# Two two-bank PSUM tiles become four one-bank tiles in a fused LSH-attention and feed-forward kernel

## The chip, the cores and the metric

One Trainium2 chip, one of its NeuronCores. The metric is the device time of one execution in microseconds (us), the median of three runs. A profiled execution gives the trace; its span runs from the first to the last instruction. Engines: PE is TensorE's matmul (PEld its weight load), DVE is VectorE, ACT is ScalarE, POOL is GpSimd, SP issues DMAs. A difference of 0.2% (1.5 us) is about what a measurement of this kernel can tell from no change.

## The reference

Attention over 2 batches of 8 heads, 768 positions of 64 numbers, in which a query sees only the keys of its own hash bucket, then two feed-forward layers over the 1536 tokens of width 512, with 2048 hidden columns each.

```python
bucket = sum((einsum(x, proj) > 0) * 2**k)                  # for q and for k, 6 bits
scores = where(q_bucket == k_bucket, q @ k.T / 8, -1e9)
x = softmax(scores) @ v                                     # [1536, 512]
h = x @ w_in;   x = maximum(0.01 * h, h) @ w_out            # layer 0
h = x @ w_in2;  y = maximum(h, 0) + alpha * minimum(h, 0)   # layer 1
out = y @ w_out2
```

## The kernel before

Every piece of work is an operation of a planner (`Plan`): it has a claim (its place in the wanted order), one or more engines that could do it with an estimated duration, and the buffers that it reads and writes. The planner simulates the engines with these estimates and emits the instructions in order of the starts that it finds. The semaphores are not the planner's: they are put in by the layer below it, tile by tile, from what each instruction reads and writes.

**Attention, about 0 to 247 us.** Eight pairs of heads. Of each pair 12 score blocks of 128 by 768 are multiplied by PE into the score tiles `sc` (L708), evicted by DVE with a minimum (L715) and raised by ACT (L718). Each score tile is `[128, 2, 512]`, two PSUM banks, and there are two of them in turn, slots 0 and 1 of the ring `s_ps`. Transposes and the product with v (L805, L814) follow. PSUM has eight banks: four in `s_ps`, two in `t_ps`, one in `o_ps`, one in `p_ps`.

**Feed-forward, about 247 us to the end.** Two layers, each in four quarters of the hidden columns (`fq`), each quarter for both batches. Weights and activations are split in a high and a low half of float16, so every product is three matmuls in a row into the same PSUM place, L1169, L1170 and L1171 in the function `three`. With 384 columns the hidden blocks `h` come out; seven products take the place of eight (`p1`, `p5`, `p2`, `p6`, `p3`, `p7`, `p4` in `h_steps`) in all but the first quarter of a layer. Six of the seven go to banks of `t_ps` or of `o_ps` and `p_ps`, and only `p2` takes a bank of `b_banks`. Then the leaky step (`leaky`), and `y_group`: four operations of three matmuls each (384 columns in layer 0, 512 in layer 1) add up one block of the second product of the quarter in a bank of `y_banks`.

**The banks that the change touches.** When the last score has been read, the two score slots are used for two tiles called `y`, of the score tiles' shape: `s_at2`. Bank 0 of tile k is `y_banks[k]`, bank 1 of tile k is `b_banks[k]`. Both lists are taken in turn. What is written there and who reads it:

- `y_banks`: the matmuls of `y_group`; read by ACT at L1300 in the first quarter, by DVE at L1303 in the others.
- `b_banks`: the product `p2`; read by DVE at L1214 (`sum_up`).
- `b_banks`: a small product at L948, by which a maximum over the partitions gets its way to all of them (`power`); read by DVE at L952. There are 16 for the weights, two for y and one for alpha.

The trace names all of these `y`. For the planner the two banks of a tile are already separate places (`Bank.use` names the bank as a span), so it gives them no common order.

Of the kernel before, what the change touches and what calls it, by code (L numbers as in the profile page):

```python
# [9 lines left out]
F32 = mybir.dt.float32  # L10
# [6 lines left out]
PSUM = bass.MemoryType.PSUM  # L17
# [30 lines left out]
class Slot:  # L48


    def __init__(self, pool, tag):
        self.pool, self.tag, self.bufs = pool, tag, []


class Buf:
# [12 lines left out]
    def put(self):  # L68

        if not self.ring:  # L70
            return None
        if self.slot:
            assert self.slot.bufs[-1] is self, self.slot.tag
            return None
        self.slot = self.ring.next()
        self.slot.bufs.append(self)
        return self.slot.bufs[-2] if len(self.slot.bufs) > 1 else None


class Ring:  # L80


    def __init__(self, slots):
        self.slots, self.n = list(slots), 0

    def next(self):
        self.n += 1
# [1 line left out]

    def new(self, shape, dtype, name):  # L90
        return Buf(self, lambda slot: slot.pool.tile(shape, dtype, tag=slot.tag, name=name))


class Op:
# [209 lines left out]
def lsh_attention_ffn_kernel(  # L304
# [36 lines left out]
    def pool(name, bufs, **kw):  # L341
        return ctx.enter_context(tc.tile_pool(name=name, bufs=bufs, **kw))

    def ring(name, n, tags=None, **kw):
        p = pool(name, 1, **kw)
        rings = [Ring([Slot(p, f"{tag}{k}") for k in range(n)]) for tag in tags or (name,)]
        return rings if tags else rings[0]

    def part(ring, *ks):
        return Ring([ring.slots[k] for k in ks])  # L350
# [1 line left out]
    const = pool("const", 1)  # L352
    xpool = pool("x", 1)

    s_ps = ring("ps_s", 2, space=PSUM)
    t_ps = ring("ps_t", 2, space=PSUM)
    o_ps = ring("ps_o", 1, space=PSUM)
    p_ps = ring("ps_p", 1, space=PSUM)
    w_r = ring("wraw", 1)
    raw_r = dict(zip("kq", ring("raw", 1, "kq")))  # L360
    nat_r = dict(zip("kq", ring("nat", 1, "kq")))
# [482 lines left out]
    class View:  # L844


        def __init__(self, buf, c0, n):
            self.buf, self.c0, self.n = buf, c0, n
# [64 lines left out]
    def bank(ring):  # L913
        return Bank(ring.new([128, 1, HALF], F32, "h"), 0)

    s_at2 = [part(s_ps, k).new([128, 2, 512], F32, "y") for k in range(2)]
    y_banks = Slots([Bank(b, 0) for b in s_at2])
    b_banks = Slots([Bank(b, 1) for b in s_at2])
    e_ps = Ring(o_ps.slots + p_ps.slots)
    wt, xs, gs = {}, {}, {}  # L920

# [503 lines left out]
```

## Time and profile before

| what | value |
|---|---|
| median of three runs | 746.21 us (745.81 to 746.28) |
| the profiled execution | 746.68 us, its span 744.7 us |
| mean granted TensorE clock | 0.99 |
| busy: PE | 709.6 us, 95% of the span |
| busy: DVE | 605.3 us, 81% |
| busy: ACT | 479.9 us, 64% |
| busy: POOL | 305.3 us, 41% |

The profiled execution is 0.47 us over the median, and 1.98 us of it lie outside the span. A busy PE is one with a matmul in flight: matmuls are pipelined, so that the row of one begins before the row of the last has ended.

### The profile page before, as it was taken

Reading aid. Unit: us, or ns where it says so; the run is one execution under the profiler, and the core shown is the slowest. Engines: PE = TensorE matmul, PEld = TensorE weight load, DVE = VectorE, ACT = ScalarE, POOL = GpSimd, SP = SyncE. Lnnn points to the kernel's source line nnn. Section 1 sums busy time; section 2 is a strip of 40 time slices with the busy share of each in tenths; the row PEclk is TensorE's granted clock in tenths of the full one; section 3 lists DMA queues with packets and bytes.
Section 4 is the critical chain, followed back from the end, with each engine's and each line's share of the span. In section 5 each row is a group of like instructions: output and inputs, shape, how many; then the busy total and the mean of one; then the engine's idle time right before and its main releaser. Section 6 shows DMA issues by size and latency. Waiting matters only on the chain.

```text
span 744.7 us, 13170 instructions
## 1 busy us (share of the span) xinstructions
PE 709.6 (95%) x4979; PEld 452.8 (61%) x4979; DVE 605.3 (81%) x1097; ACT 479.9 (64%) x907; POOL 305.3 (41%) x313
## 2 busy tenths in 40 slices
PE   7999999999995999999999999988999999999997
PEld 5778787788774665565565566554555555454443
DVE  6978787767989966789898879899989999788442
ACT  6988777788888675775656555654767655555430
POOL 2987756666373242141452224233133334221420
PEclk9999999999997999999999999999999999999999
DMA  7596686777757230330231313020032113010012
GB/s 212 132 207 155 159 196 149 153 156 132 119 121 198 85 114 1 114 114 28 86 114 58 101 70 114 28 85 2 22 107 99 57 58 114 1 56 1 28 43 99
DMA packets 109488, 72.41 MB, mean 97 GB/s; under 512 B 79137, under 2 KB 101665, under 8 KB 109425
## 3 DMA queue, kind: packets, MB, share of 16 engines
q1 hardware_dynamic: 109424, 71.57, 36.4%
q8 instruction: 39, 0.64, 0.4%
q14 instruction: 25, 0.20, 0.1%
HBM read 43.00 MB, written 3.15 MB: 62 GB/s over the span
## 4 chain that ended last, share of the span: by engine, by line
PE 77%; DVE 15%; ACT 3%; issue 2%; POOL 1%; DMA 1%; DVEq 0%; POOLq 0%; ACTq 0%
PE y L1169 11%; PE y L1171 11%; PE y L1170 11%; PE h L1169 8%; PE h L1171 8%; PE h L1170 8%; PE sc L708 7%; PE pp L734 4%; PE o L805 4%; PE o L814 4%; DVE ff L1094 3%; PE tp L537 2%; DVE s L715 2%; DVE x L1303 1%; PE bp L580 1%
## 5 line engine op out<-in xcount | busy, mean ns | idle before, releaser
L414 POOL TENSOR_TENSOR ff<-ff 128x384 f16<-128x384 f32 x128 | 136.3, 1079 | 323.6 <-ACT ff L1203 214.4
L1169 PE MATMUL y<-ff 128*128 128x384 f16 (+1 forms) x496 | 172.0, 347 | 8.7 <-DVE ff L1214 3.4
L1171 PE MATMUL y<-ff 128*128 128x384 f16 (+1 forms) x496 | 171.8, 346 | 0.0
L1170 PE MATMUL y<-ff 128*128 128x384 f16 (+1 forms) x496 | 171.8, 346 | 0.0
L1170 PEld LDWEIGHTS <-ff 128*128 128x128 f16 x912 | 89.2, 98 | 81.3 <-issue 15.2
L1169 PE MATMUL h<-ff 128*128 128x384 f16 x416 | 135.7, 326 | 2.4 <-DVE ff L1200 2.4
L1170 PE MATMUL h<-ff 128*128 128x384 f16 x416 | 135.6, 326 | 0.6 <-DVE ff L1094 0.6
L1171 PE MATMUL h<-ff 128*128 128x384 f16 x416 | 135.6, 326 | 0.0
L1171 PEld LDWEIGHTS <-ff 128*128 128x128 f16 x912 | 89.2, 98 | 70.0 <-issue 0.8
L1169 PEld LDWEIGHTS <-ff 128*128 128x128 f16 x912 | 89.2, 98 | 69.1 <-DVE biggest L952 0.8
L715 DVE TENSOR_SCALAR_CACHE_REDUCE s<-sc 128x768 f32<-128x768 f32 x96 | 90.3, 954 | 24.9 <-PE sc L708 19.4
L718 ACT ACTIVATE s<-s,mn 128x768 f32<-128x768 f32 x96 | 89.8, 937 | 4.5 <-DVE s L715 4.2
L1203 ACT CAST ff<-ff 128x384 f16<-128x384 f32 x128 | 64.8, 511 | 26.1 <-DVE ff L1200 24.2
L1303 DVE SCALAR_TENSOR_TENSOR x<-y,back,x 128x384 f32<-128x384 f32 (+1 forms) x84 | 55.8, 669 | 31.4 <-PE y L1171 30.5
L1210 ACT COPY ff<-h 128x384 f32<-128x384 f32 x72 | 34.3, 476 | 52.1 <-PE h L1171 51.2
L739 ACT COPY pt<-pp 128x384 f32<-128x384 f32 x96 | 45.6, 475 | 24.9 <-PE pp L734 24.4
L708 PE MATMUL sc<-ka,qa 128*128 128x384 f32 x192 | 56.9, 377 | 2.6 <-DVE s L715 2.4
L734 PE MATMUL pp<-ident,s 128*128 128x128 f32 x288 | 50.9, 286 | 4.2 <-ACT pt L739 3.4
L1094 DVE SCALAR_TENSOR_TENSOR ff<-ff,by 128x512 f16<-128x512 f32 (+2 forms) x54 | 50.6, 970 | 0.7 <-ACT ff L1092 0.7
L708 PE MATMUL sc<-kb,qb 76*128 76x384 f32 x192 | 49.8, 340 | 0.6 <-ACT kb L611 0.6
L1092 ACT ACTIVATE ff<-ff,by 128x512 f16<-128x512 f32 (+2 forms) x54 | 44.2, 865 | 6.8 <-DVE by L957 4.3
L814 PE MATMUL o<-pt,v 128*64 128x128 f32 x576 | 48.4, 276 | 0.0
(141 smaller groups left out, 1199.4 us busy)
## 6 DMA issues: line engine op xcount, KB each, us to landing
ff<-in_moe_w_in_dram SPq DMA_DIRECT2D x32, 512.0 KB
ff<-in_moe_w_out_dram SPq DMA_DIRECT2D x32, 512.0 KB
v<-in_v_dram SPq DMA_DIRECT2D x8, 384.0 KB
out_dram<-x SPq DMA_DIRECT2D x12, 256.0 KB
k<-in_k_dram SPq DMA_DIRECT2D x7, 384.0 KB
q<-in_q_dram SPq DMA_DIRECT2D x7, 384.0 KB
kb<-ka SPq DMA_DIRECT2D x14, 192.0 KB
qb<-qa SPq DMA_DIRECT2D x14, 192.0 KB
```

What stands on the lines that cost most here:

```text
L414: nc.gpsimd.tensor_tensor(out=o, in0=a, in1=b, op=ALU.subtract)
L708: nc.tensor.matmul(sc.t[:, h, 0:HALF], lhsT=o[a].t[0:rows, row:row + 128], rhs=o[b].t[0:rows, h * HALF:h * HALF + HALF], start=(n == 0), s ...
L715: plan.add(g, vec(1.03, lambda: nc.vector.tensor_scalar(out=s.t.rearrange("p (a b) -> p a b", a=2), in0=sc.t[:, :, 0:HALF], scalar1=FILL, ...
L718: plan.add(g, act(1.12, lambda: nc.scalar.activation(out=s.t, in_=s.t, func=AF.Exp, scale=-1.0, bias=mn.t[:, 0:1], accum_out=sm.t[:, t, j: ...
L734: nc.tensor.transpose(ps.t[:, c], s.t[:, k0:k0 + 128], ident.t)
L814: nc.tensor.matmul(ps.t[64 * j:64 * j + 64, t * 128:t * 128 + 128], lhsT=v32.t[:, j, c, :], rhs=whole(pt, t)[:, T * j + c], start=False, s ...
L1094: plan.add(claim, vec(0.2 + w * 0.00108, lambda: nc.vector.scalar_tensor_tensor(out=part(lo), in0=src(), scalar=c(), in1=part(hi), op0=ALU ...
L1169: nc.tensor.matmul(ps, lhsT=lh[0], rhs=rh[0], start=first, stop=False, skip_group_check=skip)
L1170: nc.tensor.matmul(ps, lhsT=lh[0], rhs=rh[1], start=False, stop=False, skip_group_check=skip)
L1171: nc.tensor.matmul(ps, lhsT=lh[1], rhs=rh[0], start=False, stop=last, skip_group_check=skip)
L1203: plan.add(claim, act(0.51, lambda: nc.scalar.copy(out=gh.ap(), in_=g.ap(F32))), [g.use()], [gh.use()])
L1303: plan.add(claim, vec(0.69 if l else 0.56, lambda: nc.vector.scalar_tensor_tensor(out=a(), in0=ps.ap(w), scalar=c(), in1=a(), op0=ALU.mult ...
```

## The change

The two two-bank tiles are given up. The score tiles get a pool of their own, `ps_s`, which is released when the first of the new tiles is made; then a second pool, `ps_f`, opens on the same four banks, with four tiles of one bank each. The first two are `y_banks`, the other two `b_banks`. `reuse_waits="tile"` says that a tile of the new pool waits for the users of the score tile on its own bank, not for all the pool's users. For the planner, the first use of each of the four comes behind the last uses of both score tiles (`Whole`, through `Ring.before`).

```diff
-        return self.slot.bufs[-2] if len(self.slot.bufs) > 1 else None
+        return self.slot.bufs[-2] if len(self.slot.bufs) > 1 else self.ring.before
...
+class Whole:
+    def __init__(self, ring):
+        self.ring = ring
+    @property
+    def uses(self):
+        return [use for slot in self.ring.slots for use in slot.bufs[-1].uses]
+
+class Later:
+    def __init__(self, make):
+        self.make, self.pool = make, None
+    def tile(self, *args, **kw):
+        self.pool = self.pool or self.make()
+        return self.pool.tile(*args, **kw)
...
-    s_ps = ring("ps_s", 2, space=PSUM)
     t_ps = ring("ps_t", 2, space=PSUM)
     o_ps = ring("ps_o", 1, space=PSUM)
     p_ps = ring("ps_p", 1, space=PSUM)
+    s_pool = tc.alloc_tile_pool(name="ps_s", bufs=1, space=PSUM)
+    s_ps = Ring([Slot(s_pool, f"ps_s{k}") for k in range(2)])
+
+    def single():
+        s_pool.release()
+        return ctx.enter_context(tc.tile_pool(name="ps_f", bufs=1, space=PSUM, reuse_waits="tile"))
+
+    f_pool = Later(single)
...
-    s_at2 = [part(s_ps, k).new([128, 2, 512], F32, "y") for k in range(2)]
-    y_banks = Slots([Bank(b, 0) for b in s_at2])
-    b_banks = Slots([Bank(b, 1) for b in s_at2])
+    f_at = [Ring([Slot(f_pool, f"ps_f{k}")], Whole(s_ps)).new([128, 512], F32, "y") for k in range(4)]
+    y_banks, b_banks = (Slots([Bank(b, 0) for b in f_at[k:k + 2]]) for k in (0, 2))
```

On every engine the instructions stand in the same order before and after (10,249 of them, waits aside): nothing is moved, added or left out. What differs is which semaphore 114 of the instructions wait for. Two places on PE show it.

The first is near 423 us, in layer 0. `y_3630` is the tile of banks 0 and 1 before; after, `y_3958` is a tile for y and `y_3634` one for products. `ff_3921` holds weights, `ff_3200` and `ff_3702` the operands of `p2`. Before:

```order
L1171 MATMUL y_3630<-ff_3852,ff_3921 128x384
L1169 LDWEIGHTS ff_3702
L1169 MATMUL y_3630<-ff_3200,ff_3702 128x384
L1170 LDWEIGHTS ff_3702
L1170 MATMUL y_3630<-ff_3200,ff_3702 128x384
L1171 LDWEIGHTS ff_3702
L1171 MATMUL y_3630<-ff_3200,ff_3702 128x384
L1169 LDWEIGHTS ff_3702
L1169 MATMUL y_3630<-ff_3200,ff_3702 128x384 [waits DVE_49]
```

After, with the line numbers 28 higher:

```order
L1199 MATMUL y_3958<-ff_3856,ff_3925 128x384
L1197 LDWEIGHTS ff_3706
L1197 MATMUL y_3634<-ff_3200,ff_3706 128x384 [waits DVE_49]
L1198 LDWEIGHTS ff_3706
L1198 MATMUL y_3634<-ff_3200,ff_3706 128x384
L1199 LDWEIGHTS ff_3706
L1199 MATMUL y_3634<-ff_3200,ff_3706 128x384
L1197 LDWEIGHTS ff_3706
L1197 MATMUL y_3634<-ff_3200,ff_3706 128x384
```

The first row ends a `y_group`, the rest is `p2`, in two halves of three matmuls. Before, the second half waited for DVE's read of the y block (L1303), which is in the other bank of the tile. After, the wait stands at the first half, and it is for an earlier reader of the products' own bank.

The second place is near 698 us, in layer 1, where two operations of a `y_group` (512 columns) follow the last half of a `p2`. Before:

```order
L1171 MATMUL y_3630<-ff_3615,ff_3702 128x384
L1169 LDWEIGHTS ff_3742
L1169 MATMUL y_3630<-ff_3921,ff_3742 128x512
L1170 LDWEIGHTS ff_3742
L1170 MATMUL y_3630<-ff_3921,ff_3742 128x512
L1171 LDWEIGHTS ff_3742 [waits Pool_49]
L1171 MATMUL y_3630<-ff_3921,ff_3742 128x512
L1169 LDWEIGHTS ff_3797 [waits Activation_49]
L1169 MATMUL y_3630<-ff_3921,ff_3797 128x512 [waits DVE_49]
```

After:

```order
L1199 MATMUL y_3634<-ff_3619,ff_3706 128x384
L1197 LDWEIGHTS ff_3746
L1197 MATMUL y_3958<-ff_3925,ff_3746 128x512 [waits DVE_49]
L1198 LDWEIGHTS ff_3746
L1198 MATMUL y_3958<-ff_3925,ff_3746 128x512
L1199 LDWEIGHTS ff_3746 [waits Pool_49]
L1199 MATMUL y_3958<-ff_3925,ff_3746 128x512
L1197 LDWEIGHTS ff_3801 [waits Activation_49]
L1197 MATMUL y_3958<-ff_3925,ff_3801 128x512
```

Before, the second operation of the y block waited for DVE's read of the product (L1214) in the other bank. After, the y block waits once, at its first matmul, for the last reader of its own bank. On DVE and ACT the readers change in the same way: before, a reader waited for the last matmul that had been issued into either bank of its tile, after for the last one into its own bank.

One wait becomes later. The first `y` tile to be written is that of alpha's small product (L948, near 225 us). Before, it stood on the banks of score slot 1 and waited for the last but one score eviction. After, the tiles of the new pool take the banks in the order in which they are first used, so this one gets a bank of slot 0, and waits for the last score eviction.

## Rows read from the trace of the kernel before

**Rows 1.** Windows by stage: length, then each engine's busy time (count), clock, DMA.

```profile
332.00:470.00 138.00, 135.35 (x830) 81.07 (x829) 118.94 (x197) 78.80 (x138) 46.89 (x44) 1.00 0.25 79
470.00:540.00 70.00, 64.25 (x367) 35.55 (x365) 64.56 (x108) 42.22 (x66) 18.62 (x20) 1.00 0.12 37
540.00:610.00 70.00, 69.91 (x381) 37.11 (x380) 64.33 (x107) 44.27 (x78) 23.64 (x21) 1.00 0.26 85
610.00:744.70 134.70, 126.99 (x660) 64.33 (x658) 88.44 (x149) 58.26 (x107) 37.63 (x39) 1.00 0.14 48
```

**Rows 2.** PE's waits from 290 us on: waiter, releaser, total us, times, longest.

```profile
PE y L1169 <- DVE ff L1214: 3.4, 5, 0.7
PE y L1169 <- DVE x L1303: 3.1, 5, 1.0
PE h L1169 <- DVE ff L1200: 2.4, 2, 2.0
PE y L1169 <- DVE biggest L952: 1.1, 3, 0.4
PE y L1169 <- DVE y_max L952: 0.4, 1, 0.4
```

**Rows 3.** Timeline 418.5 to 426 us: start, duration, instruction, idle before and its releaser.

```profile
418.59 0.36 PE L948 MATMUL y<-dg,ones 128*128 128x128 f32 x1
...
419.49 0.29 DVE L952 TENSOR_REDUCE biggest<-y 128x1 f32<-128x128 f32 x1 [0.55 <-PE y L1171]
419.83 0.32 PE L1169 MATMUL y<-ff 128*128 128x384 f16 x1 [0.38 <-DVE biggest L952]
...
422.11 0.33 PE L1171 MATMUL y<-ff 128*128 128x384 f16 x1
422.47 0.62 DVE L1303 SCALAR_TENSOR_TENSOR x<-y,back,x 128x384 f32<-128x384 f32 x1 [1.52 <-PE y L1171]
423.14 0.32 PE L1169 MATMUL y<-ff 128*128 128x384 f16 x1 [0.71 <-DVE x L1303]
423.30 0.32 PE L1170 MATMUL y<-ff 128*128 128x384 f16 x1
...
425.29 0.56 DVE L1214 TENSOR_TENSOR ff<-y,ff 128x384 f32<-128x384 f32 x1 [1.01 <-PE y L1171]
425.90 0.32 PE L1169 MATMUL y<-ff 128*128 128x384 f16 x1 [0.65 <-DVE ff L1214]
```

**Rows 4.** PE's timeline at two other waits for L1303.

```profile
349.02 0.32 PE L1169 MATMUL y<-ff 128*128 128x384 f16 x1 [0.41 <-DVE x L1303]
...
513.70 0.38 PE L1169 MATMUL y<-ff 128*128 128x512 f16 x1 [0.97 <-DVE x L1303]
```

**Rows 5.** Timeline 297 to 299 us, three engines.

```profile
297.43 0.29 DVE L952 TENSOR_REDUCE biggest<-y 128x1 f32<-128x128 f32 x1 [1.41 <-PE y L1171]
...
297.76 1.05 ACT L1300 ACTIVATE x<-y,back 128x384 f32<-128x384 f32 x2 [1.64 <-DVE biggest L952]
...
298.39 0.32 PE L1169 MATMUL y<-ff 128*128 128x384 f16 x1 [0.51 <-ACT x L1300]
```

**Rows 6.** PE's timeline between 475 and 483 us.

```profile
475.83 0.34 PE L1169 MATMUL y<-ff 128*128 128x384 f16 x1 [0.39 <-DVE biggest L952]
...
482.52 0.32 PE L1170 MATMUL h<-ff 128*128 128x384 f16 x1 [0.58 <-DVE ff L1094]
```

**Rows 7.** Timeline at the last scores and alpha's product, and PE's next long wait.

```profile
224.87 0.95 DVE L715 TENSOR_SCALAR_CACHE_REDUCE s<-sc 128x768 f32<-128x768 f32 x1
225.01 0.33 PE L948 MATMUL y<-dg,ones 128*128 128x128 f32 x1 [0.35 <-DVE s L715]
...
240.12 0.47 PE L948 MATMUL y<-dg,ones 128*128 128x128 f32 x1 [5.80 <-ACT dg L619]
```

**Rows 8.** Windows around that wait, columns as in rows 1.

```profile
231.90:240.10 8.20, 1.81 (x6) 1.01 (x6) 8.06 (x15) 5.94 (x10) 1.35 (x1) 0.50 1.03 302
240.10:245.50 5.40, 5.38 (x42) 4.24 (x44) 5.19 (x13) 4.04 (x7) 0.00 (x0) 0.50 0.23 68
```

More of the change, by code (lines that the diff above doesn't have):

```diff
@@ L76, in put, with __init__ @@
         self.slot.bufs.append(self)
-        return self.slot.bufs[-2] if len(self.slot.bufs) > 1 else None
+        return self.slot.bufs[-2] if len(self.slot.bufs) > 1 else self.ring.before
 class Ring:
-    def __init__(self, slots):
-        self.slots, self.n = list(slots), 0
+    def __init__(self, slots, before=None):
+        self.slots, self.n, self.before = list(slots), 0, before
     def next(self):
```

## The prediction

> **What bounds the kernel now.** I looked first at the busy shares in the table above: PE 95%, DVE 81%. An average over stages says little, so the windows by stage come next [rows 1]. From 332 us to the end, matmuls are in flight for 396.5 of 412.7 us, and only DVE between 470 and 540 us is as busy as PE (64.56 against 64.25 of 70 us). So most of the feed-forward is bound by PE, and what can be won there is the time in which PE stands. For that the third view: whom PE waits for [rows 2]. The longest sums are waits of a matmul into a `y` tile for a reader: 3.4 us for L1214, 3.1 for L1303, 1.1 and 0.4 for L952.
>
> The timeline shows what kind of wait this is [rows 3]. Take 422 to 424 us. The last matmul of the first half of `p2` starts at 422.11. DVE's L1303 has to read the y block, which was complete before `p2` began, but it starts only at 422.47, when that half of `p2` is through. Then PE's second half of `p2` starts at 423.14, when L1303 is through. PE writes bank 1, DVE reads bank 0, and each waits for the other: a round trip from PE to DVE and back. The rows around 419 and 425 us are two more. The small product L948 starts at 418.59 and lasts 0.36, but its reader L952 starts at 419.49, after the y matmuls behind it; L1214 starts at 425.29 in the same way.
>
> **What the change does, and its price.** In the built programs the order on every engine is the same, so no duration and no DMA moves. The terms are waits.
>
> *The price of one round trip.* Without a wait the next matmul starts 0.16 us after the last (423.14 to 423.30), though its row is 0.32 long [rows 3]. The idle time in brackets is counted from the end of the last row. So a wait costs PE its idle time and another 0.16: from 422.11 to 423.14 it is 1.03, less 0.16 makes 0.87, and the row says 0.71. For the wider matmuls of layer 1 I take the same 0.16.
>
> *Which waits go.* By the order of the built programs, with their waits, all five for L1214 go (3.4 us), all three for L952 `biggest` (1.1) and the one for `y_max` (0.4). Of the five for L1303 (3.1) two are for a y block's own bank and stay: those of 0.41 and 0.97 [rows 4]. That leaves 1.7 in three. Together 6.6 us of idle time in 12 waits [rows 2], and 12 times 0.16 are 1.9: **8.5 us**. With each, its reader starts earlier too; that gives DVE and ACT slack behind a PE that is ahead of them, and I price it at nothing.
>
> Here the Trainium skill can be set beside the rows. The rows show PE standing 0.71 us until a read of the other bank has ended [rows 3]. "PSUM — Partial Sum Buffer" (the section "PSUM bank collisions raise a hardware error" and the summary) says that engines must be kept apart by bank and partition quadrant, and that another bank may be read while a matmul runs. By the page the chip does not need this wait, and all 8.5 us could go; by the rows alone, one could hold that a bank's neighbour has to be left alone, and the sum would be 0. What the built program waits for decides for the first.
>
> *An indirect gain.* At 297.76 ACT's L1300 starts behind L952, which reads the other bank; both blocks were ready when L952 started, at 297.43. Without that order L1300 starts 0.33 earlier, and so does PE at 298.39, which waits for it [rows 5]: **0.3 us**. The wait of 0.41 at 349.02 stays, but its reader is behind others that come earlier. That is worth 0 to 0.57 (0.41 and 0.16); I take 0, since DVE has its own work in between.
>
> *What is given back.* Two of the twelve waits, 475.83 (0.39) and the one for `y_max` (0.4), are worth 1.1 with their 0.16. Soon behind them, at 482.52, PE waits 0.58 for L1094, a weight conversion on DVE that the change does not touch [rows 6]. PE comes there earlier and may only wait longer. Between 0 and 1.1 is lost; I take the middle, **0.5 us**.
>
> *The wait that becomes later.* Alpha's product starts at 225.01 and will wait for the last score eviction, which runs from 224.87 for 0.95 us, to 225.82, and with 0.05 from the end of a read to a matmul's start (423.09 to 423.14 in rows 3) it starts at 225.87, 0.86 later [rows 7]. Queued behind it on PE are the products with v of the last pairs and the transposes of their scores. What hides it: at 240.12 PE has waited 5.80 us for `dg`, a scale whose chain ends on DVE, and DVE is busy for 8.06 of the 8.20 us before it [rows 7, 8]. If that cover holds, the cost is **0**, and the long wait is only shorter. If the transposes' evictions on ACT carry the delay into that chain, it is up to 0.86.
>
> *The clock.* From 231.9 to 245.5 us PE has half its clock, 0.50 in the windows [rows 8], that is 1.2 GHz. PE did little before the fall, and nearly nothing until 240.1; then it worked for 5.4 us at half speed, which at the full 2.4 GHz would have been 2.7. The later wait changes what PE does just before. I take no change, and half of the 2.7, 1.4 us, both ways for the range.
>
> The sum: 8.5 + 0.3 - 0.5 - 0 = 8.3 us. Against the profiled execution, 746.7 - 8.3 = 738.4. That execution is 0.5 over the median, so I forecast 737.9 us as a median. The best of the bounds: 8.5 + 0.3 + 0.6 + 1.4 = 10.8, or 735.4. The worst: 8.3 - 0.6 - 0.9 - 1.4 = 5.4, or 740.8.
>
> **The rivals.**
>
> *DVE takes the lead away.* PE's gain before 470 us is carried only if DVE can come earlier as well. Between 470 and 610 us DVE is busy for 92% [rows 1], and PE waits there for L1200 (2.4 us in two) and L1094 [rows 2, 6]. If DVE cannot follow, what was won until then is lost: the waits of 0.71 and 0.65, two for L952 of 0.38 each, four times 0.16 and the 0.3, together 3.1, and the 1.1 near 480 us. What remains are the six behind 610 us: four of L1214 (3.4 less 0.65) and two of L1303 (1.7 less 0.71), with their 0.16 4.7 us, or 741.5. For it: the 92%. Against it: DVE's readers wait for PE too in those stretches (1.52 and 1.01 us idle in rows 3), so DVE moves with PE where there is slack, and 118.94 of 138 us before 470 is slack enough to bring 3 us along.
>
> *It does nothing.* Another wait, for the bank's own last reader, might end just as late. Then the time stays at 746.2, or with the later wait uncovered 747.1. Against it: the second half of `p2` at 423.14 would have had to wait only for L952, which began at 419.49 and took 0.29, more than 3 us earlier [rows 3].
>
> *The clock falls for longer: slower.* The place is the stretch from 231.9 to 245.5 us. If alpha's later product thins out PE's work so that the half clock goes on behind 245.5, into the dense feed-forward, each us of it costs half a us. The gain of 8.3 and another 1.5, with which it would count as slower, are used up after some 20 us; with 30 us the time is 746.2 - 8.3 + 15 = 752.9. Against it: from 240.1 on PE is busy without a break, and in every window from 332 us on the clock is 1.00 in spite of the waits [rows 1]. The Trainium skill, "TensorE: Matmul & The Clock Gate" (a second HAM failure mode: psum-queue depth-cycling), tells of a kernel that cycled through PSUM banks, idled briefly between its groups and had its clock swing between the two levels. This trace does not agree: its banks are in turn now, with idle times of 0.38 to 0.97 us between the groups [rows 3, 4], and the clock stays.
>
> **How the numbers follow.** The forecast has 0.80, DVE taking the lead 0.12, nothing 0.05, the clock 0.03. The forecast's own bounds, 735.4 to 740.8, are the range, since the others hold 2 in 10. Faster by more than 0.2% (below 744.7) are the first two: 0.92. The same: 0.05. Slower: 0.03.
>
> **What would show it.** Right: in the waits of PE the lines for L1214 and L952 `biggest` are gone and of L1303 some 1.4 us are left; the reader of a small product starts some 0.1 us after it ends, not after the y matmuls behind it; PE's busy time is nearly the same less the overlap, and the span is shorter by 8. The later wait: alpha's product has about 1.2 us idle before it in place of 0.35, and the wait of 5.80 is near 5. Wrong: PE's waits for L1200 and L1094 between 470 and 540 us grow by as much as was won (the first rival); waits of the same length under another releaser (the second); a clock of 0.50 in a window behind 250 us (the third). What I could have wrong most easily is the part that is given back, as its size comes from one row.

## The result, and the profile after

The changed kernel takes 735.34 us as a median of 4 runs (735.03 to 737.03), the kernel before 746.01 beside it (745.70 to 746.28): a ratio of 0.9861, 95% interval 0.9845 to 0.9876 (the quotient of the two medians is 0.9857). The forecast of 737.9 had the right sign and mechanism, and was 2.6 too high; 735.34 lies 0.06 below the lower end of its range. Repeated with four runs of the changed kernel and eight of the kernel before, the ratio is 0.9877 (0.986 to 0.9893), 736.84 us against 745.70. All twelve runs of the changed kernel have the median 736.8, inside the range, so of the 2.6 some 1.4 belongs to this first set of runs; the last experiments show what differs from one execution to the next. The ratios leave out one run of 1214.85 us at a mean granted clock of 0.557, among the ten of the kernel with other bank places. The first profiled execution took 735.07 us, with a span of 733.2.

First the waits of PE from 250 us on, in the changed kernel (its line numbers are 28 higher in the feed-forward and 29 in the attention):

```profile
PE h L1197 <- DVE ff L1228: 2.4, 2, 2.0
PE y L976 <- ACT dg L648: 1.5, 2, 1.0
PE y L1197 <- DVE x L1331: 1.0, 1, 1.0
PE h L1198 <- DVE ff L1122: 0.3, 1, 0.3
PE y L1197 <- ACT x L1328: 0.2, 1, 0.2
```

Against [rows 2]: the lines for the product's reader (3.4 us) and for the two small products' readers (1.1 and 0.4) are gone, the five waits for the y block's reader are one, and the wait for `h` is the same 2.4. The line for `dg` is the only one that has grown. Before, it was:

```profile
PE y L948 <- ACT dg L619: 1.0, 1, 1.0
```

The windows by stage, as in [rows 1]:

```profile
332.00:470.00 138.00, 138.00 (x853) 83.32 (x852) 121.84 (x202) 79.86 (x140) 47.55 (x45) 1.00 0.25 77
470.00:540.00 70.00, 64.94 (x370) 35.99 (x369) 66.55 (x109) 43.85 (x70) 20.15 (x20) 1.00 0.17 54
540.00:610.00 70.00, 70.00 (x379) 36.89 (x377) 64.44 (x111) 45.33 (x81) 22.10 (x22) 1.00 0.23 71
610.00:733.20 123.20, 119.16 (x625) 60.99 (x623) 82.26 (x136) 52.08 (x97) 34.26 (x36) 1.00 0.14 50
```

PE stood 2.65 us of the 138 before 470 us; now it never stands there. DVE takes more work into the same window (121.84 us, was 118.94) and so keeps up.

The place of [rows 3], 3 to 5.5 us earlier now (1.6 of them are there at the first `h` already):

```profile
415.33 0.36 PE L976 MATMUL y<-dg,ones 128*128 128x128 f32 x1
...
415.72 0.29 DVE L980 TENSOR_REDUCE biggest<-y 128x1 f32<-128x128 f32 x1
...
418.18 0.62 DVE L1331 SCALAR_TENSOR_TENSOR x<-y,back,x 128x384 f32<-128x384 f32 x1 [0.49 <-PE y L1199]
418.30 0.33 PE L1199 MATMUL y<-ff 128*128 128x384 f16 x1
418.46 0.33 PE L1197 MATMUL y<-ff 128*128 128x384 f16 x1
...
419.96 0.55 DVE L1242 TENSOR_TENSOR ff<-y,ff 128x384 f32<-128x384 f32 x1
...
420.25 0.33 PE L1199 MATMUL y<-ff 128*128 128x384 f16 x1
420.41 0.33 PE L1197 MATMUL y<-ff 128*128 128x384 f16 x1
```

The small product's reader starts 0.03 us after it ends (0.54 before). The second half of `p2` starts at 418.46, 0.16 after the matmul ahead of it, while DVE still reads the y block, which is now another tile (418.18 to 418.80). From 419.96 to 420.51 DVE reads the product while PE's matmuls into the y block's tile follow one another 0.16 apart. So a read of one bank and matmuls into another do run together, as the Trainium skill has it in "PSUM — Partial Sum Buffer" (the section "PSUM bank collisions raise a hardware error"): its rule is by bank and quadrant, and these rows agree.

### The profile page after: what moved, and what is told of

It is laid out like the page before. It is cut to its first block, busy times and chain, and to the rows that moved or that the text cites. A ratio compares the mean times of both kernels' runs of the same rounds, so it can differ in the third digit from the quotient of the medians.

```text
span 733.2 us, 13169 instructions
## 1 busy us (share of the span) xinstructions
PE 704.9 (96%) x4979; PEld 450.9 (61%) x4979; DVE 605.6 (83%) x1097; ACT 479.1 (65%) x907; POOL 304.1 (41%) x313
## 4 chain that ended last, share of the span: by engine, by line
PE 82%; DVE 12%; ACT 2%; issue 2%; DMA 1%; SPq 0%; DVEq 0%
PE y L1197 11%; PE y L1199 11%; PE y L1198 11%; PE h L1197 8%; PE h L1199 8%; PE h L1198 8%; PE sc L737 7%; PE pp L763 4%; PE o L834 4%; PE o L843 4%; DVE ff L1122 3%; PE tp L566 2%; DVE s L744 2%; PE bp L609 1%; DVE x L1183 1%
## 5 line engine op out<-in xcount | busy, mean ns | idle before, releaser
L1331 DVE SCALAR_TENSOR_TENSOR x<-y,back,x 128x384 f32<-128x384 f32 (+1 forms) x84 | 55.8, 669 | 27.1 <-PE y L1199 26.9
```

What stands on the lines that cost most here:

```text
L1331: plan.add(claim, vec(0.69 if l else 0.56, lambda: nc.vector.scalar_tensor_tensor(out=a(), in0=ps.ap(w), scalar=c(), in1=a(), op0=ALU.mult ...
```

## Experiments

**Where the time came from in the feed-forward.** The same PE instructions, matched by order in the two first profiles, show how much earlier each start comes (times and gains in us, times of the kernel before):

| at, before | gained there | what |
|---|---|---|
| 298.39 | 0.33 | the order of ACT's reader behind the small product's, [rows 5] |
| 349.02 | 0.57 | the wait of 0.41 with 0.16, [rows 4] |
| 367.67, 419.83, 475.83, 479.17 | 2.18 | four waits for a small product's reader |
| 423.14, 644.23, 674.98 | 2.23 | three waits for a y block's reader |
| 425.90, 646.66, 679.68, 698.56, 714.04 | 4.19 | five waits for a product's reader |
| 477.47, 482.52 | -0.23 | 0.55 lost to a wait for `dg`, 0.32 won at L1094 |
| 355.84, 392.89, 550.56, 576.35 | 0.70 | four small steps (-0.08, 0.28, 0.35, 0.15), no term of the prediction |
| sum | 9.97 | first `h` matmul to the end: 497.89 to 487.92, 9.97 |

**Is it the place of the banks?** The changed kernel also allots the score tiles other PSUM banks. This kernel takes only that part: the score tiles are made behind the other rings, and the two-bank tiles stay.

```diff
-    s_ps = ring("ps_s", 2, space=PSUM)
     t_ps = ring("ps_t", 2, space=PSUM)
     o_ps = ring("ps_o", 1, space=PSUM)
     p_ps = ring("ps_p", 1, space=PSUM)
+    s_ps = ring("ps_s", 2, space=PSUM)
```

> The kernel before, with the scores' pool opened behind the other three, so that the scores and the two-bank y tiles lie on banks 4 to 7 as they do after the change. Order and waits are those of before. Theory (the waits across the two banks of a tile were the cost): 746.0 us, within 0.7. Rival (the new places of the banks, or the clock that comes with them, made a part of the gain): 735 to 744 us.

Measured: 746.27 us against 746.37 (ratio 0.9998, 0.9984 to 1.0013), and 497.89 us from the first `h` to the end, as before. Within the 0.2% of this comparison, where the banks lie makes no difference.

**Half of the change each.** Two kernels split only one of the two tiles; the other stays a tile of two banks. The first splits the one with the index 0, the second the one with the index 1. The edits from here on are against the changed kernel.

```diff
-    f_at = [Ring([Slot(f_pool, f"ps_f{k}")], Whole(s_ps)).new([128, 512], F32, "y") for k in range(4)]
-    y_banks, b_banks = (Slots([Bank(b, 0) for b in f_at[k:k + 2]]) for k in (0, 2))
+    def f_tile(name, *shape):
+        return Ring([Slot(f_pool, name)], Whole(s_ps)).new([128, *shape], F32, "y")
+    y0, b0, two = f_tile("ps_fy", 512), f_tile("ps_fb", 512), f_tile("ps_f2", 2, 512)
+    y_banks = Slots([Bank(y0, 0), Bank(two, 0)])
+    b_banks = Slots([Bank(b0, 0), Bank(two, 1)])
```

(The second has `[Bank(two, 0), Bank(y1, 0)]` and `[Bank(two, 1), Bank(b1, 0)]`.)

> The change for the first pair alone: one bank each for y 0 and product bank 0, a two-bank tile for y 1 and product bank 1. Ten of the twelve waits stood at the first tile; the other two are those at 479.17 and 714.04 us, which came to 0.5 and 0.9 us. Theory: the gain of the change less 0.9 to 1.4 us, that is 736.5 to 738 us. Rival (each tile counts alike): half of the gain, 740.7 us.

> The change for the second pair alone: a two-bank tile for y 0 and product bank 0, one bank each for the other two. Theory: only the waits at 479.17 and 714.04 us go, with some at readers: 0.9 to 1.5 us, that is 744.5 to 745.1 us. Rival (each tile counts alike): 740.7 us. If the new pool itself is worth something ahead of the feed-forward, it shows here too: 743.5 to 744.3 us.

Measured: 737.27 us (0.9877, 0.9857 to 0.9897) and 744.05 (0.997, 0.9959 to 0.998), against 746.37. From the first `h` to the end they win 8.22 and 1.83 us; together 10.05, where the whole change wins 9.97. So the gains add. The waits that are left to the first, with the line numbers 32 higher than before (L1335 is L1303, L1246 is L1214, L984 is L952):

```profile
PE y L1201 <- DVE x L1335: 1.0, 1, 1.0
PE y L1201 <- DVE ff L1246: 0.7, 1, 0.7
...
PE y L1201 <- DVE y_max L984: 0.4, 1, 0.4
```

and to the second:

```profile
PE y L1201 <- DVE x L1335: 3.1, 5, 1.0
PE y L1201 <- DVE ff L1246: 2.7, 4, 0.7
...
PE y L1201 <- DVE biggest L984: 1.1, 3, 0.4
```

Each kernel keeps the cross-bank waits of the tile that it does not split. The second gained more than I had expected: its 1.83 us are the two waits (0.55 and 0.88), 0.26 at PE's wait for L1094, a weight conversion, which fell from 0.58 to 0.33 us when PE no longer waited for `y_max` ahead of it, and a small step of 0.15 at 576.35. Its 744.05 lies where I had put it if the new pool were worth something ahead of the feed-forward. But 1.83 of the 2.3 us lie behind the first `h`, and the 0.5 that is left is within the interval of the ratio (1.5 to 3.1 us in all), so that such a worth is not shown.

**Is it the tile, or that y and product share one?** Here y block shares a tile with y block, product with product; the order on every engine is the same.

```diff
-    f_at = [Ring([Slot(f_pool, f"ps_f{k}")], Whole(s_ps)).new([128, 512], F32, "y") for k in range(4)]
-    y_banks, b_banks = (Slots([Bank(b, 0) for b in f_at[k:k + 2]]) for k in (0, 2))
+    yy, bb = f_tile("ps_fy", 2, 512), f_tile("ps_fb", 2, 512)
+    y_banks, b_banks = (Slots([Bank(t, 0), Bank(t, 1)]) for t in (yy, bb))
```

> Two two-bank tiles again, but the two y banks share one and the two product banks the other. The order of the instructions is the same. A y block directly follows another one at 57 places, and there the second now waits for the first one's reader. Theory: each such place costs a part of a round trip, 0.3 to 0.87 us: 15 to 50 us over the kernel before, 761 to 796 us. Rival (it is one-bank tiles as such, or the number of tiles, that matters): between 735 and 747 us.

Measured: 769.79 us, 3.1% slower than before (1.0286 to 1.0337). Its longest waits from 240 us on (L1334 and L1331 are the y block's readers on DVE and ACT):

```profile
PE y L1200 <- DVE x L1334: 18.1, 25, 1.5
PE y L1200 <- ACT x L1331: 8.3, 11, 1.1
```

Where two y blocks follow each other, both in one tile, the new block waits for the reader of the last: 36 waits, 26.4 us, where the kernel before has six waits for these readers (3.1 and 0.5 us). I had counted 57 such places; at the others the wait is too short for the list or there is none. The price of a shared tile lies in who shares it.

**The later wait of alpha's product.** The changed kernel once more, and one in which the four tiles are made at once in their order, so that alpha's product stands on a bank of score slot 1 and waits, as before the change, for the last but one eviction. The two differ in two waits.

```diff
-    def __init__(self, make):
-        self.make, self.pool = make, None
+    def __init__(self, make, tags=()):
+        self.make, self.tags, self.made = make, tags, None
-    def tile(self, *args, **kw):
-        self.pool = self.pool or self.make()
-        return self.pool.tile(*args, **kw)
+    def tile(self, shape, dtype, tag, name):
+        if self.made is None:
+            p = self.make()
+            self.made = {t: p.tile(shape, dtype, tag=t, name=name) for t in self.tags}
+        return self.made[tag]
...
-    f_pool = Later(single)
+    f_pool = Later(single, [f"ps_f{k}" for k in range(4)])
```

> The changed kernel with the four new tiles placed so that alpha's product gets a bank of score slot 1 again and waits, as before the change, for the last but one score eviction. Two waits differ from the changed kernel, the order on every engine does not. Theory (the later wait is covered by the chain that ends in dg): the idle time before alpha's product is back near 0.35 us, the wait of 6.08 near 239.3 us is some 0.9 longer, PE's part from there on is not shifted, and the time is that of the changed kernel within 0.3 us, near 735.3. Rival (the later wait costs its 0.86): 0.9 us less than the changed kernel, near 734.5.

> The changed kernel once more, for a direct comparison with the other placement and for a second profile of the part ahead of the feed-forward. Theory (what the first profile won there, 0.8 us before 215 us and 0.8 in the stretch of half clock, is chance of one execution): the head differs from that of the first profile by up to 1 us and the time from the first h product to the end is the same 487.9 within 0.3. Rival (the change itself shortens the head): again 0.7 to 0.9 us ahead of the kernel before at 215 us and 1.6 at 246 us.

Measured, in the same set of runs: 737.00 us with the earlier wait, 736.84 with the later one. PE's timeline at alpha's product and at the next long wait, first the kernel with the earlier wait, then the changed kernel (compare [rows 7]):

```profile
225.19 0.33 PE L978 MATMUL y<-dg,ones 128*128 128x128 f32 x1 [0.35 <-DVE s L746]
...
230.39 0.55 PE L765 MATMUL pp<-ident,s 128*128 128x128 f32 x3 [0.63 <-ACT pt L770]
...
232.12 0.83 PE L765 MATMUL pp<-ident,s 128*128 128x128 f32 x3 [1.19 <-ACT pt L770]
...
233.53 0.90 PE L765 MATMUL pp<-ident,s 128*128 128x128 f32 x3 [0.57 <-ACT pt L770]
...
240.30 0.48 PE L978 MATMUL y<-dg,ones 128*128 128x128 f32 x1 [5.86 <-ACT dg L650]
```

```profile
226.02 0.33 PE L976 MATMUL y<-dg,ones 128*128 128x128 f32 x1 [1.23 <-DVE s L744]
...
231.15 0.55 PE L763 MATMUL pp<-ident,s 128*128 128x128 f32 x3 [0.57 <-ACT pt L768]
...
232.36 0.55 PE L763 MATMUL pp<-ident,s 128*128 128x128 f32 x3 [0.66 <-ACT pt L768]
...
233.47 0.55 PE L763 MATMUL pp<-ident,s 128*128 128x128 f32 x3 [0.57 <-ACT pt L768]
...
240.25 0.48 PE L976 MATMUL y<-dg,ones 128*128 128x128 f32 x1 [6.23 <-ACT dg L648]
```

The product comes 0.83 later, and 14 us behind it nothing is left of that: the next product starts at 240.30 and 240.25, the first `h` at 247.11 and 247.14. The cover held, and every profile says so: in all four of the kernel before the next product starts 15.1 us behind alpha's, in all four of the changed kernel 14.2; the 0.9 by which alpha's product is later is gone there.

Where the delay goes is harder to read from this pair, since the clock fell earlier in the first: in the window from 232.4 to 234.4 us it is 0.50 there and 1.00 in the second. So two rows of the first are longer (0.83 and 0.90, not 0.55), and its long wait of 5.86 is shorter by that. The kernel before has two more profiles in which the clock fell only behind the last of these rows. There the long wait is 6.51 and 6.52 us; the row of the second profile is:

```profile
242.12 0.48 PE L948 MATMUL y<-dg,ones 128*128 128x128 f32 x1 [6.52 <-ACT dg L619]
```

Against these, the 6.23 with the later product is some 0.28 less. So the long wait takes up a third of the delay, and PE's waits for the transposed scores' evictions on ACT ahead of it take up the rest: 0.63 and 1.19 us with the earlier product, 0.57 and 0.66 with the later one.

**The head, and the clock.** The first profile was 1.6 us ahead at the first `h` (245.24 against 246.86), with instructions and waits ahead of 225 us that are the same. Two more profiles of the changed kernel, beside the second one above, and three of the one before were taken to see whether the change does this.

> The kernel before once more, one look, for a third profile of its head. If the head's start is chance, PE's last score matmuls near 215 us stand up to 0.8 us apart from the first profile and the stretch of half clock may be 10.2 us in place of 13.7; if the kernel sets it, both are as in the first profile. From the first h product to the end 497.9 us within 0.3 in either case.

> The changed kernel, a further profile. In four profiles with one-bank products the granted clock fell to 0.50 for 3.4 us after the wait of 2.0 us near 486 us in two, which cost 0.8 us to the end; in four profiles of kernels with the two-bank tiles (the kernel before twice, and two experiments) it never fell there. Theory (the fall is chance of one execution, the wait before it being the same in both): from the first h product to the end 487.9 or 488.7, either may come. Rival (the change brings the fall): mostly 488.7.

> The kernel before, a further profile for the same question. Theory (chance): the fall after the wait of 2.0 us near 492 us may be seen here too, and then costs up to 1.7 us: 497.9 to 499.6 from the first h product to the end. Rival (the change brings it): no fall, 497.9.

> As the further profile of the changed kernel: 487.9 without a fall of the clock near 488 us, 488.7 with one.

> As the further profile of the kernel before: 497.9 without a fall of the clock near 494 us, up to 499.6 with one.

In this order they took 748.01 us (one run), 736.57 (median of two), 746.14 (of eight), 737.42 (of two) and 745.98 (of eight). By profile, in us:

| kernel, execution | product behind the long wait | first `h` | first `h` to the end |
|---|---|---|---|
| before, first | 240.12 | 246.86 | 497.89 |
| before, second | 242.12 | 248.19 | 497.90 |
| before, third | 239.59 | 245.65 | 497.91 |
| before, fourth | 239.40 | 246.14 | 497.94 |
| changed, first | 239.33 | 245.24 | 487.92 |
| changed, second | 240.25 | 247.14 | 488.72 |
| changed, third | 239.16 | 245.41 | 487.92 |
| changed, fourth | 240.86 | 247.41 | 488.72 |

The first `h` comes between 245.65 and 248.19 before and between 245.24 and 247.41 after: the head's 1.6 us is chance of an execution, and no part of the change that can be told from it. A part of this chance can be seen. Near 17 us the clock falls in some executions; here the changed kernel, first profile, then second (the clock is the third figure from the end):

```profile
17.00:21.00 4.00, 3.51 (x19) 2.61 (x18) 3.62 (x9) 3.89 (x9) 3.17 (x3) 1.00 0.02 6
17.00:21.00 4.00, 4.00 (x15) 3.61 (x16) 2.72 (x7) 3.50 (x7) 2.75 (x3) 0.57 0.12 41
```

Of the table, the second profile before and the second and fourth after have this early fall, and they are the three with the latest first `h`.

The last column has two values after the change and one before. What makes the difference shows in the windows of the changed kernel, again first profile, then second:

```profile
488.00:492.00 4.00, 4.00 (x27) 2.38 (x26) 4.00 (x7) 1.09 (x2) 2.35 (x3) 1.00 0.16 43
488.00:492.00 4.00, 4.00 (x15) 1.91 (x14) 3.96 (x7) 1.57 (x4) 2.16 (x2) 0.57 0.00 0
```

and in PE's timeline of the second:

```profile
487.90 0.32 PE L1197 MATMUL h<-ff 128*128 128x384 f16 x1 [2.02 <-DVE ff L1228]
488.06 0.32 PE L1198 MATMUL h<-ff 128*128 128x384 f16 x1
...
488.73 0.52 PE L1198 MATMUL h<-ff 128*128 128x384 f16 x1
489.05 0.52 PE L1199 MATMUL h<-ff 128*128 128x384 f16 x1
```

PE stood 2.02 us, and then the clock fell to 1.2 GHz: the matmuls from 488.41 to 491.61 stand 0.32 us apart, not 0.16. Ten of them cost 1.6 us, of which 0.8 comes back when the wait of 0.97 behind it shrinks to 0.2. Three of the five profiles with four one-bank tiles and this order have it (the changed kernel twice and the other placement once), and none of the five with the old tiles (the kernel before four times and the one with other bank places), though the same wait of 2.03 stands in them. It is not bound to one-bank tiles: behind the same wait the kernel in which like shares with like, with tiles of two banks, has it too (clock 0.57 from 504 to 508 us), and the two kernels with half of the change do not. So whether it comes depends on the execution. The three of the five that have it are also those with the early fall near 17 us; the second profile before has the early fall and none near 494. Whether the change makes the fall likelier, and whether the two falls belong together, so few profiles do not settle; this stays open.

**All four tiles in one ring.** A try at a better version: y blocks and products take any of the four in turn. The planner then chooses another order, so this is no single edit.

```diff
-    y_banks, b_banks = (Slots([Bank(b, 0) for b in f_at[k:k + 2]]) for k in (0, 2))
+    y_banks = b_banks = Slots([Bank(b, 0) for b in f_at])
```

> All four one-bank tiles in one ring, taken in turn by y blocks and by products. The planner sees other banks and moves instructions on PE, DVE, ACT and POOL, so this is no single edit. Theory (with one bank to a tile, the banks' readers are off the path): the wait of 0.97 us for a y block's own bank goes, nothing else is won, and the time is 733 to 737. Rival (the new order puts a reader of some bank back on the path, as a y block holds its bank for four operations): over 737.

Measured: 742.84 us (0.9956 of before, 0.9938 to 0.9974), 6.0 us over the changed kernel in the same set. DVE's and PE's timelines show one reason:

```profile
512.73 1.52 DVE L1035 SCALAR_TENSOR_TENSOR ff<-ff 128x1024 int32<-128x1024 int32 x1
514.28 1.23 DVE L1038 SCALAR_TENSOR_TENSOR ff<-ff 128x1024 int32<-128x1024 int32 x1
515.42 0.61 DVE L1331 SCALAR_TENSOR_TENSOR x<-y,back,x 128x384 f32<-128x384 f32 x1
```

```profile
516.08 0.59 PE L1197 MATMUL y<-ff 128*128 128x512 f16 x1 [3.79 <-DVE x L1331]
```

A bank's reader stands behind weight conversions on DVE, and PE waits 3.79 us for it; PE's matmuls behind it are long (0.59, against 0.38 ahead of the wait), at 1.2 GHz (a clock of 0.50 from 516 to 519 us). The rival was right: a reader came back on the path. How much of the 6.0 us is the wait, the clock and the rest of the new order was not tried apart.

## Why the prediction was right, and where its sizes were off

*The mechanism.* Right: the wait is one for the tile, not for the bank. The split halves take their own waits away and keep the others, the pairing of like with like brings 36 waits for a y block's reader in place of six, and the place of the banks makes no difference. The rival that nothing happens falls with it.

*The price of a round trip.* Right: the twelve waits cost 6.6 us idle and 0.16 each, predicted 8.5, and the table adds to 8.60 (2.18, 2.23 and 4.19). The 0.16 held for the wider matmuls too: the wait of 0.65 at 646.66 was worth 0.81. The indirect 0.3 was 0.33.

*The wait of 0.41 at 349.02*, taken at 0, was worth its upper bound of 0.57. My reason, that DVE has its own work in between, was wrong there, and so was the price of nothing for readers that start earlier. Before, DVE stood 0.61 us for a matmul into the other bank, and from there its work followed without a break up to the reader at 348.35 for which PE waited:

```profile
341.80 0.62 DVE L1303 SCALAR_TENSOR_TENSOR x<-y,back,x 128x384 f32<-128x384 f32 x1 [0.61 <-PE y L948]
```

After, this idle time is gone, and the reader ends before PE needs it.

*What is given back* was taken at 0.5 and is 0.23, and not where the step had it. I had PE wait longer for L1094; that wait fell from 0.58 to 0.26. The loss is 0.55 at a wait for `dg`, a chain on DVE and ACT that I had not looked at; that it is near the 0.5 is luck:

```profile
471.98 0.33 PE L976 MATMUL y<-dg,ones 128*128 128x128 f32 x1 [0.42 <-ACT dg L648]
...
476.16 0.32 PE L1198 MATMUL h<-ff 128*128 128x384 f16 x1 [0.26 <-DVE ff L1122]
```

*Four small steps*, together 0.70 us, had no term. The two largest are waits of the same kind, 0.12 us for L1303 at 392.89 and 0.09 for L1300 at 550.56, too short for the list in [rows 2]. The feed-forward's sum is then 8.60 + 0.33 + 0.57 - 0.23 + 0.70 = 9.97 us, where 8.3 was predicted.

*The later wait*: 0 was right: behind the long wait PE is at 240.25 us with it and at 240.30 without. Its cover was only in part the long wait, which shrank by some 0.28 us where the clock is the same in both (6.51 and 6.52 to 6.23); waits for ACT ahead of it took up the rest. Near 5 was forecast for the long wait in place of 5.80, and the first profile has 6.08, since the clock fell later in it.

*The clock*, taken at 0 with 1.4 both ways: around 240 us the change makes no difference that stands out from those between executions. The third rival had the wrong place, but its kind of event is there: in some executions 1.2 GHz behind a wait of 2 us near 488, at a net price of 0.8. With it the feed-forward wins 9.17, without it 9.97.

*DVE takes the lead away*: no. Its readers moved with PE, and the waits for `h` stayed at 2.4 us.

The forecast of 737.9 lies 1.1 over the twelve runs' 736.8, and 2.6 over the first four runs' median. In the feed-forward the working is 1.7 us short of the executions without the clock's fall near 488 us, and 0.9 short of those with it.

## What to carry to other kernels

When two engines wait for each other in turn, look whether the bytes are the same, or only the tile: in this kernel a semaphore is put in for the tile, and two banks can be read and written at once only if they are two tiles. Where tiles have to span two banks, it matters who shares one: a y block with a product cost 10 us of the feed-forward, a y block with the next one 34 (521.7 against 487.9 us). Such a wait costs its idle time and the overlap of the matmuls around it, here 0.36 to 1.0 us each, and the sum of them can be forecast from the list of waits. Before anything else is counted as given back, follow each chain that the earlier engine meets next; and take more than one profile of each kernel before a difference of 1 us in a stretch that the change does not touch is explained.

## What was not expected of the hardware

A wait of 2.0 us on PE within a dense stretch is followed by 1.2 GHz in some executions and by 2.4 GHz in others of the same program: 488.72 and 487.92 us from the first `h` to the end, twice each in four profiles of the changed kernel. The Trainium skill, "TensorE: Matmul & The Clock Gate" (a second HAM failure mode: psum-queue depth-cycling), ties such a swing to short idle times between groups of matmuls that cycle through PSUM banks. That does not agree here: from 332 to 470 us the groups go through their banks in turn, and the clock is 1.00 before and after the change, with 2.65 us of idle time between them and with none.
